# A new order of the work between batch 2's first score piece and its first feed-forward piece

## The chip, the cores and the metric

The kernel runs on one core of one Trainium2 chip. The metric is the device time of one execution in microseconds (us), smaller is better. A core has five engines with queues of their own: TensorE (PE, matrix products into PSUM; its weight loads are shown as PEld), VectorE (DVE), ScalarE (ACT), GpSimd (POOL) and SyncE (SP, which here only issues DMAs). Each takes its instructions in the order of the program and waits on semaphores for what the others make. PSUM has eight banks of 128 x 512 numbers in fp32.

## The reference

Four batches, eight heads, 768 tokens, 64 numbers per head. Attention, then a feed-forward layer over the heads side by side:

```python
scores = (q @ k.T) / 8                       # per batch and head
keep = causal                                # heads 0, 2, 6 ("retrieval")
keep = causal & (key < 4 | query - key < 64) # the other five ("streaming")
a = softmax(where(keep, scores, -1e9));  o = a @ v
x = o with its heads side by side            # 3072 tokens x 512
h = x @ w_in                                 # 512 x 2048
g = max(h, 0) + alpha * min(h, 0)
out = g @ w_out                              # 2048 x 512
```

## The kernel before

Products run in bf16 with fp32 sums. A batch's eight heads are four pairs, (2,6), (1,5), (0,4), (3,7), numbered n = 4 * batch + pair; batch 2 is n = 8 to 11. Tokens of the feed-forward layer come in tiles t of 512 and 256 in turn, two per batch: t = 4 and 5 belong to batch 2.

The program is one list of named items, `ORDER` (line 14). The loop at line 817 calls each item's function in that order, and so sets the order in every engine's queue; a planner wrote the list offline. An item is named by a letter, then n, head of the pair (0 or 1) and piece, or t and block:

- `Lq`, `Lk`, `Lv`: loads from HBM, issued by SP (two parts of Lk13 by POOL). `Cq`, `Ck`, `Cv`: casts to bf16, in batch 2 and later on DVE (lines 322, 341, 356). `Dq`, `Dk`: DMA transposes of the cast q and k, issued by SP (lines 329, 345).
- `S`: a score piece on PE; `s`: its exponential on ACT (lines 477, 524, 526); `m`: its mask by a product on DVE (lines 486, 535, 538). A retrieval head of batch 2 has six pieces of 448 columns, a streaming head two of 352 and one of 448.
- `A`: weights times v on PE (line 562), with the row sums; `a`: the division on DVE (lines 572, 573); `X`: a DMA transpose of the pair's result into `xT`, issued by SP (line 581).
- `P`: a piece of x @ w_in on PE, four matmuls of 512 columns or eight of 256 (line 607), the last in each sum reading the fourth pair's `xT`; `p`: ACT's relu into one of three `neg` buffers (line 612); `g`: DVE's product and sum that makes g (line 619; t even one instruction, t odd two).
- `O`: a quarter of g @ w_out for 128 tokens, four matmuls of 512 columns (line 627); `o`: ACT's copy (line 633) and the store, issued by POOL (line 637).

Score items that stand near one another are collected and emitted together (`emit_burst`, line 425). If each of the pair's heads has at least 576 columns in the collection, the heads go on the two halves of the array's rows and run side by side (line 438); otherwise each piece goes alone over all rows, against zeros in the other half (line 431). An item that `beside_burst` (line 442) does not let pass ends the collection.

PSUM banks are handed out in the list's order too: `take` (line 151) picks the bank that was given back longest ago, `give` (line 157) returns it. So another order gives other banks to the items, and a PE item waits until the bank's last reader has run.

In the stage that the change touches, PE does the last four P of t = 2 and 3, the scores and the `A` of batch 2, and the O of t = 2 and 3; the next item, P4.11, needs `xT` of n = 8 to 11. The loads and casts for batch 3 (n = 12 to 15) have begun.

Of the kernel before, what the change touches and what calls it, by code (L numbers as in the profile page):

```python
# [40 lines left out]
p2.9 P3.4 Ck9 Cq9 g2.9 P2.14 p2.14 g2.14 Cq8 p3.4 Lq10 Lq11 Dk8.0 P2.10 p2.10 Dk9.1 o1.0 p2.3  # L41
g2.3 g3.4 Dk8.1 P3.2 P3.14 P3.12 P2.8 Dq8 P2.1 P3.8 o1.1 p3.2 Dk9.0 Lv10 g2.10 Dq9 p3.14 P2.7
Ck10 g3.2 p3.12 g3.12 g3.14 P2.2 p2.2 g2.2 Cq10 Dq10 P2.11 p2.1 g2.1 p2.11 p2.8 g2.11 P3.6 P2.5
p2.5 g2.5 P2.13 p2.13 g2.8 g2.13 P2.0 p2.0 g2.0 p2.7 P3.0 p3.0 P2.4 S8.0.5 Lv8 Lv11 P2.15 P2.12
s8.0.5 Cq11 g3.0 p2.15 g2.7 g2.15 S8.0.0 p2.12 g2.12 Ck11 p3.6 S9.0.2 P2.6 p2.6 g3.6 s8.0.0 p2.4 g2.4
g2.6 s9.0.2 p3.8 P3.10 g3.8 p3.10 O3.0.0 O2.0.0 S8.1.5 s8.1.5 O3.0.1 O2.0.1 g3.10 m8.0.0 Cv8 S8.1.3 S9.0.0 S8.0.3
S9.1.1 S8.0.1 S9.1.0 s8.1.3 s9.1.0 s8.0.1 s9.0.0 s8.0.3 m8.0.3 m8.0.1 O2.0.2 O2.0.3 o2.0 Dk10.1 Lv9 m9.0.0 Cv9 m8.0.5
Dk11.0 m9.1.0 m9.0.2 S8.0.4 S9.0.1 S10.1.1 S8.1.4 Dq11 s8.1.4 Lq13 Lk13 O3.0.2 Dk10.0 s9.1.1 s10.1.1 s9.0.1 s8.0.4 O3.0.3
o3.0 Dk11.1 S10.1.0 S10.1.2 m9.0.1 S11.0.2 S9.1.2 S8.0.2 S11.0.0 s9.1.2 Cv10 m9.1.1 A9.0 s11.0.2 s10.1.0 O2.3.0 m9.1.2 A9.1
a9.0 a9.1 X9 s10.1.2 s11.0.0 O2.3.1 Lq15 Lv14 Lq12 S8.1.0 S11.0.1 S10.0.3 m10.1.0 s8.0.2 S10.0.1 S8.1.2 S8.1.1 S10.0.0  # L50
O2.3.2 s8.1.2 s8.1.0 m8.1.4 Cq13 s11.0.1 s8.1.1 m11.0.2 m10.1.2 m8.0.4 m11.0.0 A8.0 s10.0.0 m8.1.5 m10.1.1 O2.3.3 a8.0 S11.1.2
S10.0.4 S11.1.0 S10.0.5 S10.0.2 m8.1.3 m11.0.1 s10.0.3 s10.0.1 S11.1.1 s11.1.2 A10.1 s11.1.1 O2.2.0 O2.1.0 s10.0.4 m6.0.2 m10.0.1 Cv11
m8.1.1 m8.1.0 a10.1 m10.0.4 Ck13 m10.0.0 m11.1.2 A11.0 A8.1 O2.1.1 s10.0.2 s10.0.5 o2.3 s11.1.0 Dk13.0 m11.1.1 m10.0.3 m10.0.5
m11.1.0 A10.0 a11.0 a8.1 a10.0 O3.1.0 A11.1 Cq12 O2.2.1 O2.2.2 O2.2.3 a11.1 X8 O2.1.2 O3.1.1 O3.1.2 X10 o2.2
O3.1.3 O2.1.3 X11 P4.11 o2.1 P4.14 P5.14 p5.14 P4.4 P4.6 Lk12 P5.0 g5.14 Ck12 p4.4 p4.6 p4.11 P4.13
g4.6 p4.14 g4.11 Lq14 g4.14 P5.12 P4.5 P4.12 p4.13 Dq12 o3.1 p5.0 g4.13 Cq14 g5.0 Dk13.1 p4.5 g4.5
g4.4 Cv14 P4.9 p4.9 g4.9 P4.2 P5.2 Dq13 p5.12 g5.12 P4.10 p5.2 P4.8 P4.1 p4.12 g4.12 g5.2 p4.10
g4.10 Lv15 Dk12.0 Dk12.1 Lv12 p4.1 Lk14 Lv13 Lk15 g4.1 P4.7 P4.0 p4.2 g4.2 p4.8 g4.8 p4.0 p4.7
# [799 lines left out]
```

## Time and profile before

| what | value |
| --- | --- |
| median of 3 runs | 227.11 us (226.39 to 227.92) |
| profiled execution | 226.45 us |
| its span, first to last instruction | 224.7 us |
| changed stage, first score piece to P4.11 | 97.25 to 129.93 us of the span |

Times in the profile are us from the span's start, means of a group are ns. A timeline row is: start, us that the group took, engine and line, operation, what it writes and reads, shape, count. A q behind an engine's name means its sequencer, which issues DMAs. Matmuls overlap, so the end of one lies behind the start of the next; from start to start is what each costs PE. A `DMA_TRANSPOSE` row gives the time of issuing; the data land later.

### The profile page before, as it was taken

To read this page: it belongs to the slowest core of one execution; us is meant where nothing else is said; L and a number is where in the kernel's file an instruction comes from. 1 tells how busy PE (TensorE), PEld (TensorE's weight loads), DVE (VectorE), ACT (ScalarE), POOL (GpSimd) and SP (SyncE) were. 2 spreads that over 40 slices of the span, in tenths; PEclk is the share of its full clock that TensorE was granted. 3 is DMA by queue.
4 is the path that set the end of the run, shared out by engine and by line. 5 is a ranking of instruction groups with operands and counts; after the bars stand their busy time and mean duration, and the time that the engine had idled before them with its cause. 6 is when DMAs were issued, how large, how long until landed. Compare 5 with 4: busy or idle time off the path is not lost.

```text
span 224.7 us, 5206 instructions
## 1 busy us (share of the span) xinstructions
PE 220.6 (98%) x1986; PEld 135.7 (60%) x1986; DVE 148.4 (66%) x395; ACT 139.5 (62%) x286; POOL 45.0 (20%) x91
## 2 busy tenths in 40 slices
PE   7999999999999999999999999999999999999995
PEld 7989876575556557564556455556556455664454
DVE  5799648995579618898799029977589226866000
ACT  3788668999898037577993137787584237563311
POOL 4678769400230001000401001000110110000000
PEclk9999999999999999999999999999999999999999
DMA  6999999999999999999979898995721620000213
GB/s 194 309 235 203 272 218 266 220 196 202 221 233 233 160 248 217 187 172 202 240 164 183 218 238 195 191 161 115 126 95 39 152 96 0 0 1 3 91 63 128
DMA packets 96185, 37.58 MB, mean 167 GB/s; under 512 B 83208, under 2 KB 94368, under 8 KB 96160
## 3 DMA queue, kind: packets, MB, share of 16 engines
q1 hardware_dynamic: 89904, 27.92, 66.1%
q0 software_dynamic: 5792, 8.93, 18.0%
q10 hardware_dynamic: 464, 0.40, 0.6%
q8 instruction: 15, 0.25, 0.5%
q14 instruction: 10, 0.08, 0.1%
HBM read 27.71 MB, written 6.29 MB: 151 GB/s over the span
## 4 chain that ended last, share of the span: by engine, by line
PE 98%; DVE 0%; issue 0%; DVEq 0%
PE P L607 37%; PE P L627 36%; PE P L562 7%; PE P L438 4%; PE P L421 3%; PE P L698 3%; PE P L371 2%; PE P L646 2%; PE P L431 1%; PE P L508 1%; PE P L587 1%; PE P L470 0%; PE P L369 0%; DVE kT L394 0%; DVE ot L655 0%
## 5 line engine op out<-in xcount | busy, mean ns | idle before, releaser
L619 DVE SCALAR_TENSOR_TENSOR g<-neg,oma,P 128x256 bf16<-128x256 f32 (+1 forms) x128 | 71.0, 610 | 41.4 <-ACT neg L612 40.8
L607 PE MATMUL P<-xT,w_in_b 128*128 128x512 bf16 (+1 forms) x512 | 86.6, 326 | 0.0
L627 PE MATMUL P<-w_out_b,g 128*128 128x512 bf16 x368 | 85.1, 380 | 0.0
L612 ACT ACTIVATE neg<-P 128x512 f32<-128x512 f32 x96 | 54.2, 601 | 26.3 <-PE P L607 20.9
L607 PEld LDWEIGHTS <-w_in_b 128*128 128x128 bf16 x512 | 49.4, 98 | 32.4 <-DVE g L619 0.2
L627 PEld LDWEIGHTS <-g 128*128 128x128 bf16 x368 | 33.9, 98 | 37.4 <-issue 0.9
L477 ACT ACTIVATE eR<-P 128x448 bf16<-128x448 f32 (+3 forms) x63 | 35.9, 616 | 5.4 <-PE P L438 2.5
L633 ACT COPY ot<-P 128x512 f32<-128x512 f32 x23 | 13.8, 600 | 36.9 <-PE P L627 31.4
L637 POOL DMA_DIRECT2D out_dram<-ot x18 | 10.3, 572 | 110.2 <-ACT ot L633 110.0
L524 ACT ACTIVATE eS<-P 128x352 bf16<-128x352 f32 x45 | 20.5, 481 | 3.6 <-PE P L438 3.2
L573 DVE TENSOR_TENSOR xn<-P,rcp 128x448 bf16<-128x448 f32 (+1 forms) x32 | 19.1, 595 | 1.1
L535 DVE TENSOR_TENSOR eS<-eS,ms_near 128x352 bf16<-128x352 bf16 x45 | 14.7, 338 | 0.8 <-ACT eS L524 0.6
L486 DVE TENSOR_TENSOR eR<-eR,mr_near 128x128 bf16<-128x128 bf16 x54 | 10.9, 231 | 3.9 <-ACT eR L477 3.7
L421 PE MATMUL P<-qT,kT 128*128 128x192 bf16 (+14 forms) x68 | 11.2, 251 | 0.2 <-DVE kT L394 0.2
L562 PEld LDWEIGHTS <-eS 128*128 128x128 bf16 x266 | 9.8, 97 | 2.4 <-issue 0.6
L562 PE MATMUL P<-vb,eS 128*128 128x65 bf16 x266 | 11.0, 193 | 0.0
L572 DVE RECIPROCAL rcp<-P 128x7 f32<-128x7 f32 (+1 forms) x32 | 6.3, 196 | 6.6 <-PE P L562 6.0
L438 PEld LDWEIGHTS <-kT 64*128 64x128 bf16 x167 | 6.7, 94 | 6.1 <-issue 5.5
L438 PE MATMUL P<-qT,kT 64*128 64x176 bf16 (+7 forms) x167 | 10.3, 251 | 0.0
L562 PE MATMUL P<-vb,eR 128*128 128x65 bf16 x258 | 9.9, 193 | 0.0
L655 DVE COPY ot<-P 128x128 f32<-128x128 f32 x1 | 0.3, 292 | 14.3 <-PE P L646 14.3
L562 PEld LDWEIGHTS <-eR 128*128 128x128 bf16 x258 | 9.0, 97 | 1.1
(96 smaller groups left out, 175.0 us busy)
## 6 DMA issues: line engine op xcount, KB each, us to landing
out_dram<-ot POOLq DMA_DIRECT2D x18, 256.0 KB, 3.8
kf<-in_k_dram SPq DMA_DIRECT2D x21, 192.0 KB
qf<-in_q_dram SPq DMA_DIRECT2D x18, 192.0 KB
vf<-in_v_dram SPq DMA_DIRECT2D x14, 196.0 KB
qf<-in_q_dram SPq DMA_DIRECT2D x7, 384.0 KB
vf<-in_v_dram SPq DMA_DIRECT2D x12, 192.0 KB
w_in_b<-in_moe_w_in_dram POOLq DMA_DIRECT2D x8, 256.0 KB, 9.4
w_out_b<-in_moe_w_out_dram POOLq DMA_DIRECT2D x4, 512.0 KB, 13.3
```

Of the source, the lines that this page charges most:

```text
L421: nc.tensor.matmul(to, keys, queries, start=True, stop=stop)
L438: nc.tensor.matmul(to, keys[own], queries[own], start=True, stop=True)
L477: nc.scalar.activation(ebuf[n, hh][:, lo:hi].rearrange("p (x c) -> p x c", x=len(parts)), P[:, got[0]:got[0] + len(parts), 0:(hi - lo) // ...
L524: nc.scalar.activation(slots, sc[:, 0:352].rearrange("p (s c) -> p s c", c=176), AF.Exp, scale=scale)
L535: nc.vector.tensor_tensor(slots, slots, ms_near[:, 0:2, :] if m == 0 else ms_near[:, 1:3, :], op=ALU.mult)
L562: nc.tensor.matmul(pav[:, i, :], e[:, o:o + 128], vv[:, j, hh, 0:D + 1], start=(m == 0), stop=(m == len(terms) - 1))
L573: nc.vector.tensor_tensor(xn[n][:, 0:nt, D * hh:D * hh + D], pav[:, :, 0:D], rcp.to_broadcast([128, nt, D]), op=ALU.mult)
L607: nc.tensor.matmul(psg[:, w * i:w * (i + 1)], w_in_b[:, c, 128 * fb:128 * (fb + 1)], xT[:, c, o:o + w], start=(x == 0), stop=(x == 3))
L612: nc.scalar.activation(neg[t, f], bank(held["P", t, f][0]), AF.Relu, scale=-1.0)
L619: nc.vector.scalar_tensor_tensor(g_buf[t % 2][:, fb, 0:w], neg[t, f][:, c], oma[:, fb:fb + 1], bank(got[0])[:, c], op0=ALU.mult, op1=ALU.add)
L627: nc.tensor.matmul(bank(held["O", t, s][0]), g_buf[t % 2][:, f, 128 * s:128 * (s + 1)], w_out_b[:, f, :], start=(f == 0), stop=(f == 15))
L633: nc.scalar.copy(ot, bank(got[0]))
```

## The change

The list is changed from S8.0.5, the first score item of batch 2, to the last O ahead of P4.11: 188 items. Both lists hold the same items, each once, and the functions are the same. According to its description the order was sought by a planner that takes transposes and loads to land 1.5 (us) late. On PE the two lists read as follows, with score pieces that are emitted together in brackets and those side by side on the halves marked by "|":

```
before: [8.0.5] P2.15 P2.12 [8.0.0] [9.0.2] P2.6 P3.10 O3.0.0 O2.0.0 [8.1.5] O3.0.1 O2.0.1
  [9.0.0 8.0.3 8.0.1 | 8.1.3 9.1.1 9.1.0] O2.0.2 O2.0.3 [8.0.4 9.0.1 | 10.1.1 8.1.4] O3.0.2 O3.0.3
  [11.0.2 8.0.2 11.0.0 | 10.1.0 10.1.2 9.1.2] A9.0 O2.3.0 A9.1 O2.3.1
  [11.0.1 10.0.3 10.0.1 10.0.0 | 8.1.0 8.1.2 8.1.1] O2.3.2 A8.0 O2.3.3
  [10.0.4 10.0.5 10.0.2 | 11.1.2 11.1.0 11.1.1] A10.1 O2.2.0 O2.1.0 A11.0 A8.1 O2.1.1 A10.0 O3.1.0
  A11.1 O2.2.1 O2.2.2 O2.2.3 O2.1.2 O3.1.1 O3.1.2 O3.1.3 O2.1.3 P4.11
after:  [8.0.1] P2.6 P3.10 [9.0.0] P2.12 P2.15 O2.0.0 O2.0.1 O2.0.2
  [8.0.0 9.0.2 8.0.4 | 9.1.0 8.1.3 9.1.1] O2.0.3 O3.0.0 O3.0.1 O3.0.2 O3.0.3
  [9.0.1 8.0.3 8.0.2 | 8.1.1 9.1.2 8.1.0] O2.3.0 A9.0 O2.3.1
  [8.0.5 11.0.1 11.0.0 11.0.2 | 8.1.5 10.1.0 10.1.2] O2.3.2 O2.3.3 A9.1 O2.2.0 A8.0
  [10.0.1 10.0.3 10.0.0 | 8.1.4 10.1.1 8.1.2] O2.2.1 O2.2.2
  [10.0.5 10.0.4 10.0.2 | 11.1.0 11.1.2 11.1.1] A10.1 A8.1 O3.1.0 O3.1.1 A10.0 A11.1 A11.0
  O2.1.0 O2.2.3 O2.1.1 O2.1.2 O2.1.3 O3.1.2 O3.1.3 P4.11
```

SP issues in both lists Lv8, Lv11, Dk10.1, Lv9, Dk11.0, Dq11, Lq13, Lk13, Dk10.0, Dk11.1; then before X9, Lq15, Lv14, Lq12, Dk13.0, X8, X10, X11, and after Lq15, Lv14, Lq12, Dk13.0, X8, X9, X10, X11. The new lines:

```diff
+p2.5 g2.5 P2.13 p2.13 g2.8 g2.13 P2.0 p2.0 g2.0 p2.7 P3.0 p3.0 P2.4 S8.0.1 g3.0 P2.6 P3.10 p3.6
+Lv8 g2.7 S9.0.0 p2.4 Lv11 m6.0.2 g2.4 p2.6 s8.0.1 Dk10.1 P2.12 s9.0.0 P2.15 g2.6 O2.0.0 O2.0.1 m9.0.0 Lv9
+O2.0.2 S8.0.0 p3.8 g3.8 S9.0.2 p2.12 g2.12 S9.1.0 S8.1.3 p3.10 g3.10 S8.0.4 g3.6 p2.15 g2.15 S9.1.1 s9.1.1 Ck11
+s9.0.2 Cv10 Dk11.0 O2.0.3 Cq11 Dq11 O3.0.0 s8.1.3 O3.0.1 o2.0 Lq13 Lk13 s8.0.4 Dk10.0 Dk11.1 s8.0.0 s9.1.0 O3.0.2
+O3.0.3 o3.0 m9.0.2 S9.0.1 S8.0.3 m9.1.1 Lq15 S8.1.1 S9.1.2 S8.1.0 S8.0.2 s9.0.1 Cv9 s8.1.1 O2.3.0 m9.0.1 A9.0 m8.0.0
+O2.3.1 Lv14 Cv11 a9.0 S8.0.5 S11.0.1 s8.1.0 S11.0.0 m8.1.0 s9.1.2 S8.1.5 s8.0.3 S10.1.0 m9.1.2 m8.1.3 m8.1.1 s8.0.2 S10.1.2
+S11.0.2 s8.0.5 m8.0.3 s8.1.5 s10.1.0 O2.3.2 s11.0.2 O2.3.3 m8.0.5 Cv8 s11.0.1 m9.1.0 A9.1 m8.0.4 o2.3 O2.2.0 m8.0.1 A8.0
+s11.0.0 S8.1.4 S10.1.1 a9.1 s10.1.2 S10.0.1 S10.0.3 m10.1.2 S10.0.0 S8.1.2 s8.1.4 s10.0.3 s8.1.2 s10.0.0 m8.1.5 O2.2.1 a8.0 O2.2.2
+S10.0.5 m11.0.1 s10.1.1 S10.0.4 m10.1.0 s10.0.1 S10.0.2 S11.1.0 m11.0.2 S11.1.2 m10.0.3 Lq12 S11.1.1 s10.0.5 m10.1.1 A10.1 m8.1.4 m10.0.0
+A8.1 s11.1.0 Ck13 m11.1.0 m10.0.5 s11.1.2 m11.1.2 Dk13.0 a8.1 s10.0.4 X8 O3.1.0 m10.0.4 O3.1.1 m10.0.1 s10.0.2 s11.1.1 A10.0
+m11.1.1 X9 A11.1 m11.0.0 A11.0 a10.1 O2.1.0 O2.2.3 O2.1.1 o2.2 O2.1.2 a10.0 X10 a11.1 a11.0 X11 O2.1.3 Cq12
+Cq13 O3.1.2 O3.1.3 P4.11 o2.1 P4.14 P5.14 p5.14 P4.4 P4.6 Lk12 P5.0 g5.14 Ck12 p4.4 p4.6 p4.11 P4.13
```

More of the change, by code (lines that the diff above doesn't have):

```diff
@@ L43 @@
 Ck10 g3.2 p3.12 g3.12 g3.14 P2.2 p2.2 g2.2 Cq10 Dq10 P2.11 p2.1 g2.1 p2.11 p2.8 g2.11 P3.6 P2.5
[L44 to L52, printed above, removed]
@@ L53 @@
-m8.1.1 m8.1.0 a10.1 m10.0.4 Ck13 m10.0.0 m11.1.2 A11.0 A8.1 O2.1.1 s10.0.2 s10.0.5 o2.3 s11.1.0 Dk13.0 m11.1.1 m10.0.3 m10.0.5
-m11.1.0 A10.0 a11.0 a8.1 a10.0 O3.1.0 A11.1 Cq12 O2.2.1 O2.2.2 O2.2.3 a11.1 X8 O2.1.2 O3.1.1 O3.1.2 X10 o2.2
-O3.1.3 O2.1.3 X11 P4.11 o2.1 P4.14 P5.14 p5.14 P4.4 P4.6 Lk12 P5.0 g5.14 Ck12 p4.4 p4.6 p4.11 P4.13
+p2.5 g2.5 P2.13 p2.13 g2.8 g2.13 P2.0 p2.0 g2.0 p2.7 P3.0 p3.0 P2.4 S8.0.1 g3.0 P2.6 P3.10 p3.6
+Lv8 g2.7 S9.0.0 p2.4 Lv11 m6.0.2 g2.4 p2.6 s8.0.1 Dk10.1 P2.12 s9.0.0 P2.15 g2.6 O2.0.0 O2.0.1 m9.0.0 Lv9
```

## The prediction

> **What bounds the kernel now.** I read the page's head first: span, busy times, clock, chain.
>
> ```profile
> span 224.7 us, 5206 instructions
> PE 220.6 (98%) x1986; PEld 135.7 (60%) x1986; DVE 148.4 (66%) x395; ACT 139.5 (62%) x286; POOL 45.0 (20%) x91
> PEclk9999999999999999999999999999999999999999
> PE 98%; DVE 0%; issue 0%; DVEq 0%
> ```
>
> TensorE (PE) is busy 98% of the span, at the full granted clock in every slice, and the chain that ended last is PE's own queue. The profiled execution took 226.45 us: 224.7 of span and 1.75 around it, 0.66 below the median of 227.11.
>
> A busy PE could still hide gaps, because the ends of matmuls are modelled. So I read starts, in PE's timeline over the changed stage, from batch 2's first score piece (97.25) to its first feed-forward piece (129.93).
>
> ```profile
> 97.25 0.36 PE L431 MATMUL P<-qT,kT 128*128 128x64 bf16 x3
> 97.44 1.89 PE L607 MATMUL P<-xT,w_in_b 128*128 128x512 bf16 x8
> ...
> 105.06 0.71 PE L438 MATMUL P<-qT,kT 64*128 64x176 bf16 x12
> 105.70 1.90 PE L627 MATMUL P<-w_out_b,g 128*128 128x512 bf16 x8
> 107.53 0.52 PE L438 MATMUL P<-qT,kT 64*128 64x128 bf16 x8
> 107.98 1.90 PE L627 MATMUL P<-w_out_b,g 128*128 128x512 bf16 x8
> 109.82 0.71 PE L438 MATMUL P<-qT,kT 64*128 64x176 bf16 x14
> 110.46 0.57 PE L562 MATMUL P<-vb,eS 128*128 128x65 bf16 x13
> 110.87 1.03 PE L627 MATMUL P<-w_out_b,g 128*128 128x512 bf16 x4
> ...
> 113.08 0.90 PE L438 MATMUL P<-qT,kT 64*128 64x176 bf16 x11
> 113.91 1.04 PE L627 MATMUL P<-w_out_b,g 128*128 128x512 bf16 x4
> ...
> 116.38 0.75 PE L438 MATMUL P<-qT,kT 64*128 64x128 bf16 x13
> 117.05 0.63 PE L562 MATMUL P<-vb,eS 128*128 128x65 bf16 x15
> ...
> 123.03 7.07 PE L627 MATMUL P<-w_out_b,g 128*128 128x512 bf16 x32
> 129.93 5.25 PE L607 MATMUL P<-xT,w_in_b 128*128 128x512 bf16 x31
> ```
>
> From one group's start to the next is what the group costs. The last 32 matmuls of 512 columns take 129.93 - 123.03 = 6.90 us, 0.216 each, or four (a quarter O or a piece P) in 0.863. From 97.44, eight take 1.73. An AV of 13 matmuls takes 110.87 - 110.46 = 0.41. No row carries a wait, and the starts join without a hole: in 32.68 us I find no wait of PE. **So no wait can be taken out here**; the order can only change PE's own work, or bring waits in.
>
> The Trainium skill would let one doubt this. "TensorE: Matmul & The Clock Gate", section "Back-to-back issue gap", gives about 131 ns per 512-column matmul in a stream of weight loads and matmuls, and "Perfetto Trace Analysis", "Identifying the Most-Contended Engine", asks to judge headroom by weight-load busy time, here 60%. By the first, each 0.863 would hide 0.34 us. The trace speaks against it: 0.216 is the least step between these matmuls, with no wait before them.
>
> **The change part by part.** All 188 items of the stage stay, so every instruction is there as before, DMAs too. Only places change.
>
> *Score pieces in pairs.* Neighbouring score items are emitted together, head 0 and head 1 on the two halves of the array if each has 576 columns. A full-attention piece has 448 columns; a streaming one 352 (pieces 0 and 1) or 448 (piece 2). The longer half sets the time. Before, the five paired groups have longer halves of 1248, 800, 1248, 1696 and 1344 columns and take 0.64, 0.45, 0.64, 0.83 and 0.67 us by the rows above: 0.11 + 0.424 per thousand columns. After, there are again five, of 1344, 1344, 1600, 1344 and 1344 (the first is 8.0.0, 8.0.4, 9.0.2 against 9.1.0, 8.1.3, 9.1.1). The sum goes from 6336 to 6976 columns: +0.27. Each paired group also costs the work ahead of it 0.10 (eight O from 105.70 to 107.53 take 1.83, not 1.73), five times before and after; a group of 1344 so takes 0.78 in all. Unpaired remain 448 + 352 columns in place of four times 448, at 0.19 (97.44 - 97.25) per 448: 0.76 becomes 0.34, -0.42. **PE's work: -0.15 us.** All else on PE costs the same wherever it stands.
>
> *The start: does VectorE (DVE) keep up?*
>
> ```profile
> 94.67 2.72 DVE L619 SCALAR_TENSOR_TENSOR g<-neg,oma,P 128x512 bf16<-128x512 f32 x4
> 101.25 3.90 DVE L619 SCALAR_TENSOR_TENSOR g<-neg,oma,P 128x256 bf16<-128x256 f32 x8
> 95.71 1.70 ACT L612 ACTIVATE neg<-P 128x512 f32<-128x512 f32 x3 [0.27 <-PE P L607]
> ```
> ```profile
> L535 DVE TENSOR_TENSOR eS<-eS,ms_near 128x352 bf16<-128x352 bf16 x45 | 14.7, 338 | 0.8 <-ACT eS L524 0.6
> ```
>
> A g of 512 columns costs DVE 0.68; the second row holds three split ones and two whole, so a split one costs 0.85. PE now runs S8.0.1, P2.6, P3.10, S9.0.0, P2.12, P2.15 and three O2.0 by 97.25 + 0.19 + 0.15 + 7 x 0.863 = 103.6, and meets the first pair group there; before, it met its first at 105.06. Its last piece, S9.1.1, takes the PSUM bank that g3.6 gives back. On DVE, from 97.4, g3.0, g2.7, g2.4, g2.6, a mask, g3.8, g2.12, g3.10 and g3.6 come to 4 x 0.85 + 4 x 0.68 + 0.34 = 6.5, at 103.9; the three neg buffers make ACT wait for DVE now and then, and by following these relus through I add 0.3: 104.2. PE asks at 104.1 (0.1 of entry, two 176-wide matmuls and a piece of 448 ahead on that half). A wait of 0 to 0.3 us; I take 0.1. Behind it on PE all else waits. O2.0.3 needs g2.15 for its fourth matmul alone, at 103.6 + 0.78 + 0.65 = 105.0; g2.15 is done at 104.9. Covered by little: 0 to 0.2, I take 0.
>
> *The middle: transposes of item 11.* Ck11 moves behind g2.15 on DVE, and SyncE's (SP's) queue waits for it with Dk11.0, Dq11 and the loads Lq13, Lk13 behind.
>
> ```profile
> 73.38 5.11 SPq L581 DMA_TRANSPOSE xT<-xn  x3
> 97.86 2.04 SPq L345 DMA_TRANSPOSE kT<-natk  x1
> 101.95 1.27 SPq L345 DMA_TRANSPOSE kT<-natk  x1
> 103.32 1.23 SPq L329 DMA_TRANSPOSE qT<-natq  x1
> 122.10 4.23 SPq L581 DMA_TRANSPOSE xT<-xn  x3
> 126.38 1.16 SPq L253 DMA_DIRECT2D kf<-in_k_dram  x2
> ```
> ```profile
> 79.91 4.28 PE L607 MATMUL P<-xT,w_in_b 128*128 128x512 bf16 x23
> ```
>
> SP's rows are the time to issue; the page shows no landing for them. An upper bound: batch 1's last three xT transposes were issued by 78.49, and the piece that needs the last in its fourth matmul, at 79.91 + 0.65 = 80.56, did not wait; landing came at most 2.07 us after the issue's end, at least 0. In the new order Ck11 ends about 105.5, Dk11.0 and Dq11 end their issue at 108.0 (1.27 + 1.23), at worst at 109.6 (2.04 each), and land by 110.1 to 111.7. S11.0.1 asks at about 111.9: behind the first pair group (from 103.6, 0.78) come O2.0.3, four quarters of O3.0, a pair group, O2.3.0, A9.0 and O2.3.1, or 7 x 0.863 + 0.78 + 0.41 = 7.2, and in its own group 0.3 of entry and S8.0.5. **Cost 0**, cover 0.2 us at the bound and 1.8 with a landing at the issue's end. SP's earlier idle time costs nothing; Lq13 and Lk13 feed Cq13 and Ck13, some 10 us later.
>
> *The end of the scores.* From the fourth pair group PE does 0.78, two O, 0.78, A10.1 (15 matmuls at 0.41 / 13, 0.47), A8.1 (21, 0.66) and two O before A10.0: 6.1 us. ACT has eleven exponentials there.
>
> ```profile
> 114.88 1.88 ACT L477 ACTIVATE eR<-P 128x448 bf16<-128x448 f32 x4
> ```
>
> At 0.47 each, 0.15 for the second part of s11.1.2, and 0.45 until the first can start (entry, one piece, and 0.15 that I estimate for the hand-over): 5.8. A11.1, 0.65 later on PE, needs the twelfth and its mask: 6.6 against 6.75. A wait of 0 to 0.3 us; I take 0.05.
>
> *The tail: X11 under less cover.* P4.11 needs all four xT. Before, X8, X10 and X11 were issued by 126.33 and P4.11's fourth matmul came at 130.58. Now X9 no longer goes ahead alone at 113.2 but stands second of four in a row, and behind A11.0 come seven quarters of O (6.04 us); before, eight came behind A11.1. With P4.11 still near 129.95, A11.0 ends at 123.9. On DVE the last four outputs follow one another:
>
> ```profile
> 121.51 0.56 DVE L573 TENSOR_TENSOR xn<-P,rcp 128x384 bf16<-128x384 f32 x1
> 122.20 0.56 DVE L573 TENSOR_TENSOR xn<-P,rcp 128x384 bf16<-128x384 f32 x1
> ```
>
> At 0.7 apiece (122.20 - 121.51), from about 122.8 for a10.1, a11.0 ends at 125.6. SP reaches X8 when a8.1 is done, near 122.4, and at 4.23 / 3 = 1.41 each ends X11's issue at 128.0. It lands between 128.0 and 130.1, needed at 130.6. **Cost 0**, but 1.7 us of cover are spent. Lk12, next on SP, starts 1.7 later. Its user is Ck12 on DVE:
>
> ```profile
> 134.15 0.62 DVE L341 CAST natk<-kf 128x896 bf16<-128x896 f32 x1
> kf<-in_k_dram POOLq DMA_DIRECT2D x2, 7.0 KB, 4.1
> ```
>
> With 4.1 us to land, the only row for a load of k, its second half would be there at 132.8. Covered.
>
> **Sum:** -0.15 + 0.1 + 0 + 0.05 + 0 = 0.0. The profiled execution stays at 226.4 to 226.5, and the median at **227.1 us**. The three runs differ by 1.5 us, so under 1% (2.3 us) a measurement can hardly tell a change from none.
>
> **The rivals.** *Late transposes: slower.* For: X11 has 0.5 us of cover at the bound, Dq11 0.2, and SP's issue time has outliers, 2.04 against 1.27; at batch 1's mean of 5.11 / 3 = 1.70, X11 would end its issue at 129.2 and could land 0.7 too late. Should each of the four X take 2.04, X11 ends its issue at 130.6 and lands by 132.6: P4.11 waits 2.0 us, 229.1. It decides from X11 landing after 130.6. Against: batch 2's own three took 1.41 each, and the bound on landing is not what a landing takes. If Dq11 is late by 1.5 besides, 230.6. Chance 0.12.
>
> *DVE and ACT fall behind.* The three small waits at their upper ends: 0.3 + 0.2 + 0.3 - 0.15 = +0.65, 227.8. For: the covers are some 0.1 us; against: they were added up with the relus' waits in. Chance 0.2.
>
> *Hidden headroom.* If PE had room that its rows don't show, or if runs above the profiled one carry late DMAs that the new order bears better, up to 0.7 us (227.11 - 226.45) goes: 226.3. Since no wait stands in the trace, it gets 0.08. By the page's 131 ns the stage's 28 quarter O and P would hold 28 x 0.34 = 9.5 us, and up to 217.6 could be reached; against a step of 0.216 that never shrinks I give this 0.01, within the 0.08. The same holds for an order that bears delays of 1.5 us better but meets none: it ends as the forecast.
>
> **How the numbers follow.** Forecast, within 0.4 us of 227.1: 0.6; the others as given. The range runs from the headroom case, 226.2, to 228.5, which takes in the busy engines and the smaller delays and leaves out some 0.1 to 0.15. Slower by over 1% needs over 2.3 us of waits, the upper part of the first rival: 0.07. Faster by over 1% would need PE to do less: 0.02. Within: 0.91.
>
> **What would show it.** PE's starts again without holes over a stage 32.5 to 33 us long; five pair groups, the third the longest at 0.79; SP's four X in a row to about 128; PE at P4.11 without a wait. A wait ahead of S9.1.1 up to 0.3 shows the first term. The prediction is wrong if PE stands over 1 us, at P4.11 for xT or in the third pair group for qT, or if a later stage waits for Lk12's successors.

## The result and the profile after

The changed kernel takes 228.26 us (median of 12 runs, 227.15 to 229.84) against 226.69 us for the kernel before (12 runs, 226.16 to 228.24): ratio 1.0062, 95% interval 1.0034 to 1.0091, so about 1.4 us slower. A ratio, here and below, leaves out runs that fell in a slower state of the chip, while a median counts all runs of a kernel. Its profiled execution took 228.50 us, 226.8 of it span. The head of its page and the chain's shares:

```profile
span 226.8 us, 5207 instructions
...
PE 221.4 (98%) x1986; PEld 136.4 (60%) x1986; DVE 148.9 (66%) x395; ACT 139.7 (62%) x286; POOL 45.2 (20%) x91
...
PE 91%; DMA 3%; SPq 2%; ACT 2%; issue 1%; DVE 1%; DVEq 0%
```

PE's busy share still reads 98%. The last line is the telling one: before, the chain was PE for 98%; now it leaves PE for 3% of DMA and 2% of SP's queue. The waits of PE say where (line, releaser, us in all, times, longest):

```profile
PE P L438 <- DMA kT<-natk: 1.3, 1, 1.3
PE P L698 <- DVE busy L295: 1.2, 1, 1.2
```

The second is at the start of the program, outside the stage. The first is the only wait in the stage that the view names. PE's timeline of the stage, in the columns used ahead of the prediction:

```profile
97.88 0.35 PE L431 MATMUL P<-qT,kT 128*128 128x320 bf16 x2
...
104.38 0.92 PE L438 MATMUL P<-qT,kT 64*128 64x448 bf16 x12
105.23 4.49 PE L627 MATMUL P<-w_out_b,g 128*128 128x512 bf16 x20
109.65 0.75 PE L438 MATMUL P<-qT,kT 64*128 64x176 bf16 x11
110.33 1.04 PE L627 MATMUL P<-w_out_b,g 128*128 128x512 bf16 x4
...
112.56 0.86 PE L438 MATMUL P<-qT,kT 64*128 64x64 bf16 x18
113.35 1.90 PE L627 MATMUL P<-w_out_b,g 128*128 128x512 bf16 x8
...
116.34 0.80 PE L562 MATMUL P<-vb,eR 128*128 128x65 bf16 x21
118.42 0.74 PE L438 MATMUL P<-qT,kT 64*128 64x320 bf16 x10 [1.29 <-DMA kT<-natk]
119.10 1.90 PE L627 MATMUL P<-w_out_b,g 128*128 128x512 bf16 x8
120.93 0.75 PE L438 MATMUL P<-qT,kT 64*128 64x64 bf16 x13
121.61 0.63 PE L562 MATMUL P<-vb,eS 128*128 128x65 bf16 x15
...
131.91 2.27 PE L607 MATMUL P<-xT,w_in_b 128*128 128x512 bf16 x11
```

The stage now takes 131.91 - 97.88 = 34.03 us against 32.68, **1.35 more**, and one row carries it: the fourth paired group (8.1.4, 10.0.1 and their fellows) stands 1.29 us for a kT. From P4.11 to the end the two kernels take the same, 94.9 and 94.8 us. The rest of the difference of the two spans, 0.63 us, lies ahead of the stage (it starts at 97.88, not 97.25), where the lists are the same; it is no work of the change. Where a profile below has such an offset (the experiments e1, e2 and e8 have one of 2 to 4 us), stages are compared, not spans.

Which kT it is, and why so late, the chain tells in order of time (start, us, what):

```profile
108.71 0.58 SPq L219
...
109.34 0.65 SPq L219
...
110.04 0.96 SPq L246
...
111.04 1.21 SPq L246
...
112.29 6.09 DMA kT<-natk
...
118.42 0.74 PE P L438 x7
```

Ahead of the transpose stand the four loads of item 13, Lq13 and Lk13 (lines 219 and 246). The first transpose behind them is **Dk10.0**: 6.09 us from the start of its issue to its landing. SP's queue, after and then before:

```profile
102.47 0.43 SPq L249 DMA_DIRECT2D vf<-in_v_dram  x1
106.10 1.22 SPq L345 DMA_TRANSPOSE kT<-natk  x1
107.43 1.22 SPq L329 DMA_TRANSPOSE qT<-natq  x1
108.71 1.29 SPq L219 DMA_DIRECT2D qf<-in_q_dram  x2
110.04 2.21 SPq L246 DMA_DIRECT2D kf<-in_k_dram  x2
112.29 2.01 SPq L345 DMA_TRANSPOSE kT<-natk  x1
```
```profile
104.60 1.17 SPq L219 DMA_DIRECT2D qf<-in_q_dram  x2
105.81 1.12 SPq L246 DMA_DIRECT2D kf<-in_k_dram  x2
106.98 3.06 SPq L345 DMA_TRANSPOSE kT<-natk  x2
```

The order in the queue is that of before. But SP stands idle from 102.90 to 106.10, for Ck11; the four loads take 3.50 us to issue instead of 2.29; and Dk10.0, which before began its issue 9.73 us into the stage, begins it at 14.41. The page lists no landings, but the trace has the semaphore update at the end of each transfer, and from these the table is read (us from the stage's start):

| Dk10.0 | issue | landing | lag behind the issue's end | wanted by PE at |
| --- | --- | --- | --- | --- |
| before | 9.73 to 11.45 | 13.94 | 2.49 | 15.9 |
| after | 14.41 to 16.42 | 20.49 | 4.07 | 19.2 |

So PE wants it 3.3 us later than before and gets it 6.5 later.

### The profile page after: what moved, and what is told of

It is laid out like the page before. It is cut to its first block, busy times and chain, and to the rows that moved or that the text cites. A ratio compares the mean times of both kernels' runs of the same rounds, so it can differ in the third digit from the quotient of the medians.

```text
span 226.8 us, 5207 instructions
## 1 busy us (share of the span) xinstructions
PE 221.4 (98%) x1986; PEld 136.4 (60%) x1986; DVE 148.9 (66%) x395; ACT 139.7 (62%) x286; POOL 45.2 (20%) x91
## 4 chain that ended last, share of the span: by engine, by line
PE 91%; DMA 3%; SPq 2%; ACT 2%; issue 1%; DVE 1%; DVEq 0%
PE P L607 37%; PE P L627 32%; PE P L562 7%; PE P L438 4%; DMA kT<-natk 3%; PE P L698 3%; PE P L421 2%; PE P L371 2%; PE P L646 2%; PE P L431 1%; SPq L246 1%; ACT eR L477 1%; PE P L508 1%; PE P L587 1%; PE P L369 1%
## 5 line engine op out<-in xcount | busy, mean ns | idle before, releaser
L438 PE MATMUL P<-qT,kT 64*128 64x176 bf16 (+7 forms) x173 | 10.8, 250 | 1.3 <-DMA kT<-natk 1.3
```

The costliest lines, as they stand in the source:

```text
L438: nc.tensor.matmul(to, keys[own], queries[own], start=True, stop=True)
```

## The experiments

The theory (A in the expectations): the loss is one wait, for Dk10.0, and Dk10.0 is late because it stands on SP behind the stop for Ck11 and behind item 13's loads. The rivals: the late start of the stage's transposes is only a symptom, and the time is in other terms (the first group's bank, X11's lost cover, the DMA traffic of POOL). All edits are moves in the list, against the changed kernel unless said otherwise.

**e1.** Dk10.0 alone goes ahead of the stop:

```diff
-O2.0.2 S8.0.0 p3.8 ... Lq13 Lk13 s8.0.4 Dk10.0 Dk11.1
+Dk10.0 O2.0.2 S8.0.0 p3.8 ... Lq13 Lk13 s8.0.4 Dk11.1
```

> The changed order with one item moved: Dk10.0, the transpose whose late landing PE waited 1.29 us for at 118.42, is issued right behind Lv9, where SP stood idle from 102.9 to 106.1. Theory A (SP's queue: Ck11 late on DVE holds SP, and Dk10.0 stands behind it and four loads): Dk10.0 lands near 107, the wait ahead of S10.0.1 is gone, and the ratio to before falls from 1.006 to 0.998 to 1.001. Theory B (DMA traffic: any transpose issued among these loads and stores lands late): the wait moves to Dk11.0 or Dq11, which now start behind one transpose more, and the third pair group waits 0.5 us or more; ratio 1.003 or more. Theory C (the order itself asks PE for more than the old one did, the wait is only where it shows): the ratio stays above 1.004.

Measured: 227.29 against 227.29 us, ratio 1.0001 (0.9975 to 1.0027). The loss is gone. Dk10.0 lands 8.46 us into the stage, the stage takes 32.66 us, and in PE's timeline the fourth group follows A8.0 at once:

```profile
119.57 0.80 PE L562 MATMUL P<-vb,eR 128*128 128x65 bf16 x21
120.30 0.74 PE L438 MATMUL P<-qT,kT 64*128 64x320 bf16 x10
...
134.88 1.35 PE L607 MATMUL P<-xT,w_in_b 128*128 128x512 bf16 x6 [0.30 <-DMA xT<-xn]
```

From A8.0 to the group are 0.73 us; in the changed kernel 118.42 - 116.34 = 2.08, so the wait cost 1.35 net, the whole of the stage's growth. The last row shows what the wait had hidden: without it, P4.11's fourth matmul is 0.3 us too early for X11, which lands at 33.73.

**e2.** The loads go behind both transposes instead:

```diff
-Lq13 Lk13 s8.0.4 Dk10.0 Dk11.1 s8.0.0
+s8.0.4 Dk10.0 Dk11.1 Lq13 Lk13 s8.0.0
```

> The changed order with Lq13 and Lk13 issued behind Dk10.0 and Dk11.1 instead of ahead of them; Ck11 stays late on DVE. Theory A: Dk10.0 is issued near 108.7 instead of 112.3, lands by 113.5, and PE, which asks at 117.1, does not wait; ratio 0.998 to 1.001. If the late Ck11 alone were the cause and the four loads had no part in it, the wait would stay at over 0.8 us and the ratio at 1.004 or more. Cq13 and Ck13 have time: their loads come 3 us later and are read at 121.6 or later.

Measured: 232.18 us (median of six), ratio 1.0134 (1.0072 to 1.0196; it counts the runs of 228.92, 229.63 and 231.71): a miss. The wait for Dk10.0 is gone as foreseen (landing at 15.13, stage 32.66), but SP and its transfers are now behind for the rest of the stage (X11's issue ends at 33.53, against 31.17 in e1), and the X transposes at its end pay. PE's timeline at P4.11, and the window behind it (span, us, then busy us and count of PE, PEld, DVE, ACT, POOL, then the granted clock, DMA share, GB/s):

```profile
134.46 0.38 PE L607 MATMUL P<-xT,w_in_b 128*128 128x512 bf16 x1 [1.03 <-DMA xT<-xn]
136.80 9.53 PE L607 MATMUL P<-xT,w_in_b 128*128 128x512 bf16 x41 [1.96 <-DMA xT<-xn]
```
```profile
137.00:145.00 8.00, 7.95 (x32) 3.97 (x32) 2.24 (x5) 2.33 (x5) 0.00 (x0) 0.65 1.05 202
```

X10 and X11 land at 34.25 and 36.58; PE stands 1.03 + 1.96 us, and then has the clock at half for 6.83 us (135.82 to 142.65), which is some 3.4 us more. From P4.11 to the end are 101.0 us instead of 94.9. This profiled execution was the slowest of the six, 235.55 us; how much of these waits and of the half clock the three counted runs had, no trace shows. The backlog was only moved, and to a place with less cover.

**e3.** The stop itself is taken away, Ck11 and Cq11 cast early on VectorE:

```diff
-O2.0.2 S8.0.0 p3.8 ... s9.1.1 Ck11 ... O2.0.3 Cq11 Dq11
+O2.0.2 Ck11 Cq11 S8.0.0 p3.8 ... s9.1.1 ... O2.0.3 Dq11
```

> The changed order with Ck11 and Cq11 ahead of the first pair group, so that DVE makes them near 101.5 instead of 105.5 and SP goes on without a stop; SP's order stays. Theory A: Dk10.0 is issued near 109 and lands by 114.5, no wait for it. DVE's relu products come 1.0 us later, so S9.1.1 waits for g3.6's bank some 0.8 us longer: ratio 1.001 to 1.004. If the four loads ahead were the whole cause, the wait for Dk10.0 would still be there in part, and the ratio 1.006 or more.

Measured: 228.05 us, ratio 1.0041 (1.0009 to 1.0074). Dk10.0 lands at 15.20 and nobody waits for it; but the casts push the g of the relus back on VectorE, and PE's waits have a new line:

```profile
PE P L438 <- DVE g L619: 0.8, 1, 0.8
```

It is the bank of g3.6 ahead of S9.1.1, the wait that the prediction had at 0.1. The stage takes 33.43 us. One wait was exchanged for another, as expected.

**e4.** The opposite: in the kernel *before*, Ck11 alone is put late:

```diff
-g2.12 Ck11 p3.6
+g2.12 p3.6
-m8.0.0 Cv8
+m8.0.0 Ck11 Cv8
```

> The kernel before with one item moved: Ck11 on DVE from ahead of p3.6 (100.7) to behind m8.0.0 (105.3), as late as the changed order has it. Theory A: SP stands from 101.9 to 106; Dk11.0, Dq11, Lq13, Lk13 and Dk10.0 follow 4 us later than before. Dq11 lands near 111, S11.0.2 asks at 109.8: a wait of 1 to 1.5 us; Dk10.0 lands near 116 to 118, S10.0.3 asks at 113.1 plus that wait: 2 to 3 us more. In all +3 to +4.5 us, ratio 1.013 to 1.020. Theories B and C expect under 1 us, since neither the traffic nor PE's order is new.

Measured: 235.82 us (median of four), ratio 1.0309 (1.0237 to 1.0382; it counts the runs of 232.88, the profiled one, and 235.25), more than the 1.013 to 1.020 expected. The mechanism is made in the old order, where Dk10.0 is wanted 3.3 us sooner. PE's timeline, the chain's row of the transpose, and the window behind the wait:

```profile
113.58 0.36 PE L438 MATMUL P<-qT,kT 64*128 64x176 bf16 x3
118.19 1.30 PE L438 MATMUL P<-qT,kT 64*128 64x64 bf16 x8 [4.25 <-DMA kT<-natk]
```
```profile
112.00 6.15 DMA kT<-natk
```
```profile
118.00:123.00 5.00, 4.81 (x42) 2.31 (x44) 0.83 (x4) 3.13 (x7) 0.00 (x0) 0.66 1.10 222
```

The stage takes 38.87 us, 6.2 more than before: 4.5 us of waits and the half clock behind them (3.41 us, 117.95 to 121.36, some 1.7 us lost). The expectation had the wait and not the clock.

**e5.** The loads go into SP's idle time ahead of the stop:

```diff
-O2.0.2 S8.0.0 p3.8 ... o2.0 Lq13 Lk13 s8.0.4 Dk10.0
+Lq13 Lk13 O2.0.2 S8.0.0 p3.8 ... o2.0 s8.0.4 Dk10.0
```

> The changed order with Lq13 and Lk13 issued ahead of Dk11.0, into the stop that SP makes while it waits for Ck11; Dk10.0 keeps its place behind Dq11 and so is issued 3.5 us sooner. If what counts is SP's queue time alone, every transpose is as early as or earlier than in the changed order: Dk10.0 is issued near 10.8 us after the stage's start and lands by 15.5, no wait for it (PE asks at 19.2), the xT transposes are not later, and the ratio is 0.998 to 1.002. If a load right ahead delays what lands behind it, Dk11.0 and Dq11 land 1 us or more later than 11.2 and 13.5 after the stage's start, S11.0.1 (14.5) waits up to 1 us, and the ratio is 1.002 to 1.006.

Measured: 226.98 against 226.99 us, ratio 0.9996 (0.9976 to 1.0017). Dk10.0 lands at 14.57; Dk11.0 and Dq11, now behind the loads, land 1.0 and 0.2 later than in the changed kernel and are still in time. The stage takes 32.66. Its one wait is that of e1, at P4.11: 0.3 us for X11.

**e6.** e1, with X9 also issued early (behind O2.2.2), so that X11 has one transpose fewer ahead:

```diff
-O2.2.1 a8.0 O2.2.2 S10.0.5 ... m11.1.1 X9 A11.1
+O2.2.1 a8.0 O2.2.2 X9 S10.0.5 ... m11.1.1 A11.1
```

> The changed order with Dk10.0 right behind Lv9 as in the first experiment, and X9 ahead of Lq12 instead of behind X8, so that three transposes of xT and not four stand in a row at the end. X11 is issued some 1.2 us sooner and lands before P4.11's fourth matmul asks for it (in the first experiment it was 0.3 us late there). Stage 32.6 to 32.8 us, no wait at P4.11; ratio 0.997 to 1.000. If the four in a row are not what made X11 late, a wait of 0.2 to 0.5 us stays, ratio 1.000 to 1.002.

Measured: 226.79 against 226.99 us, ratio 0.9984 (0.9964 to 1.0004). The time fits, the reason given only in part: X11's issue ends at 30.25, 0.9 sooner than in e1, but it takes 3.22 us more to land and is there at 33.47. From start to start of the matmuls, P4.11's fourth comes 0.20 us late, against 0.46 in e1. (The waits of PE in e6 name 0.6 us for an xT; that one is at 81.16, ahead of the stage, and not of this edit.)

**e7 and e10.** The same kernel, run once (e7) and ten times (e10): the two stores of o2.0 and o3.0 are left out, so two blocks of the output are not written.

```diff
-        (nc.gpsimd if t < 6 else nc.sync).dma_start(out[r:r + 128, :], ot)
+        if (t, s) not in ((2, 0), (3, 0)):
+            (nc.gpsimd if t < 6 else nc.sync).dma_start(out[r:r + 128, :], ot)
```

> The changed order without the stores o2.0 and o3.0 (two of the 24 blocks of the output are not written; all else is done). In the changed order they move 0.5 MB at 107.4 and 110.6, while Dk10.0 waits its turn. If they are what makes Dk10.0 land 4.1 us after its issue ends instead of 2.5 as before, the wait ahead of S10.0.1 falls from 1.29 to under 0.3 us. If SP's late start and its loads are the cause, the wait stays at 0.9 us or more.

> The seventh kernel once more, timed: the changed order without the stores o2.0 and o3.0 (two blocks of the output are not written). If its one look was no accident, PE does not wait for Dk10.0 and the ratio to before is 0.998 to 1.003; if the stores have no part, it is 1.005 or more, as for the changed order.

Measured: e7 227.73 us in its one run; e10 227.18 against 227.00 us, ratio 1.0002 (0.9977 to 1.0027). PE does not wait for Dk10.0 in either (from A8.0 to the group 117.00 - 116.27 = 0.73 in e7). In e7's one run P4.11 waits 0.59 us for X11 instead, in e10 it does not. So the wait falls, as the first of e7's two branches said, but not for its reason, since the lag stays (below); that 0.9 us or more of the wait would stay is a miss. POOL's DMAs in the changed kernel, in the kernel before and in e10:

```profile
107.44 0.91 POOL L637 DMA_DIRECT2D out_dram<-ot  x1 [19.36 <-ACT ot L633]
108.34 1.27 POOL L249 DMA_DIRECT2D kf<-in_k_dram  x2
110.64 0.59 POOL L637 DMA_DIRECT2D out_dram<-ot  x1 [1.02 <-ACT ot L633]
```
```profile
108.52 0.54 POOL L637 DMA_DIRECT2D out_dram<-ot  x1 [21.07 <-ACT ot L633]
109.21 1.56 POOL L249 DMA_DIRECT2D kf<-in_k_dram  x2 [0.15 <-issue]
110.95 0.59 POOL L637 DMA_DIRECT2D out_dram<-ot  x1 [0.19 <-issue]
```
```profile
87.18 1.41 POOL L249 DMA_DIRECT2D kf<-in_k_dram  x2 [0.15 <-issue]
```

In the changed kernel POOL's DMAs go out while SP issues item 13's loads (108.71 to 112.25); before, they went out when those were through (106.93). The edit moves more than the stores: item 13's small k loads stand behind the first store on POOL, and with it gone they leave 20 us sooner. With both out of the way, SP issues its four loads in 2.3 us again, and the two transposes behind them in 2.9:

```profile
107.66 1.16 SPq L219 DMA_DIRECT2D qf<-in_q_dram  x2
108.86 1.12 SPq L246 DMA_DIRECT2D kf<-in_k_dram  x2
110.03 2.92 SPq L345 DMA_TRANSPOSE kT<-natk  x2
```

Dk10.0 lands at 18.7 (e7) and 18.8 (e10), 1.7 us sooner. Its lag behind the issue's end stays, at 3.94 and 4.06 us, so that part does not come from POOL's DMAs. The Trainium skill, "DMA: Bandwidth & Descriptors", section "Issuing engines are not separate DMA queues", says that DMAs started by different engines share the same DMA engines, and that spreading them saves only sequencer time. The runs agree that the queues are not independent, and add that the sequencer's own time suffered here: a pair of k loads took SP 1.12 us beside nothing of POOL's and 2.21 beside it. POOL is not the only thing that lengthens it: the four loads took 3.6 us in e2 and 3.0 in e5 while POOL issued nothing.

**e8 and e9.** e5 with X9 early as in e6, and the same with the store o2.2 moved behind P4.11:

```diff
-O2.2.1 a8.0 O2.2.2 S10.0.5 ... m11.1.1 X9 A11.1
+O2.2.1 a8.0 O2.2.2 X9 S10.0.5 ... m11.1.1 A11.1
-O2.1.1 o2.2 O2.1.2 ... O3.1.3 P4.11 o2.1
+O2.1.1 O2.1.2 ... O3.1.3 P4.11 o2.2 o2.1
```

> The changed order with Lq13 and Lk13 in SP's stop, as in the fifth experiment, and X9 ahead of Lq12, where that experiment left SP idle for 2.3 us (20.8 to 23.0 after the stage's start) until Ck13. So nothing behind X9 starts later, and X11 is issued about 1 us sooner than in the fifth. If X11's place in SP's queue sets its landing, it lands by 32.7 after the stage's start, PE asks at 33.3, no wait at P4.11; ratio 0.996 to 0.999. If something beside it (the store o2.2, issued at 29.4) sets it, X11 still lands at 33.4 or later and the wait of 0.2 to 0.6 us stays.

> As the eighth, with o2.2 (copy and store of 256 KB) behind P4.11, so that no store runs beside the xT transposes. If the store delays them, X11 lands 0.7 to 1.5 us after its issue ends less late than in the eighth (there 2.5 to 3.2 after the end), and the wait at P4.11 is gone for sure; ratio 0.996 to 0.999. If not, both are alike within 0.001.

Measured: e8 227.24 against 227.00 us, ratio 1.0002 (0.9968 to 1.0036); e9 226.85, ratio 0.9984 (0.9955 to 1.0012). On ACT and POOL nothing stands between the two places of o2.2, so the store left as before and e9 is a repeat of e8; it says nothing on the store. In both the stage is free of waits and 32.66 us long, and X11 lands at 31.27 (e8) and 32.54 (e9). So X11 came in time, as e8's first branch said, but e8's ratio is not under 0.999. In e9's timeline of PE:

```profile
116.22 0.80 PE L562 MATMUL P<-vb,eR 128*128 128x65 bf16 x21
116.95 0.74 PE L438 MATMUL P<-qT,kT 64*128 64x320 bf16 x10
...
130.42 0.81 PE L607 MATMUL P<-xT,w_in_b 128*128 128x512 bf16 x3
```

This is the new order with every wait taken out, and it ends where the kernel before ends. No version tried beats the kernel before by more than its interval.

What is shown: the loss is the wait for Dk10.0 (e1), and that wait is a sum against its cover. Taking away any one of the stop (e3), the loads ahead (e2, e5; in e1 the stop too) or POOL's DMAs beside them (e7, e10) is enough to end it.

Why the transpose's lag was 4.07 us here and 2.49 before is in part open. It was 3.6 to 4.1 behind the loads in e3, e4, e7 and e10, and 2.3, 2.9 and 1.6 with no load just ahead (e1, e2, e5), but before has the loads ahead too. The landings say where the difference lies. In all twelve traces the full-size transfers of SP (those with 16 updates of their semaphore) land in the order of their issue. The last load ahead landed 1.9 us after Dk10.0's issue ended in both kernels (at 13.36 before, at 18.32 after); Dk10.0 landed 0.6 us behind it before and 2.2 behind it after. So the 1.6 us more do not come from the loads ahead; they lie between the last load's landing and Dk10.0's. There, at 18.08, the changed kernel's trace has a packet of 16 KB that it calls "instruction" (queue q8, 15 of them in a run). Every one of the twelve traces has one between 15.2 and 18.8 us of the stage, and there one transfer lands 1.8 to 2.7 us behind the one ahead of it; half of the other transfers that stood in the queue near there land within 0.9 us of the one ahead. Before, it met Dk11.1 (2.4), which PE did not wait for. That this packet holds the transpose up is argued, not shown: no run moves it, and e3's Dk10.0 landed 2.05 behind its load without one.

## Why the prediction was wrong, point by point

The forecast of no change missed a small loss; 228.26 is 1.16 us above the forecast and inside the range, and +0.62% is inside the 1% that was called hard to tell.

**The step that failed** is the end of the middle part: "SP's earlier idle time costs nothing; Lq13 and Lk13 feed Cq13 and Ck13, some 10 us later". Behind SP's stop it followed Dk11.0, Dq11 and the two loads, and ended there. Dk10.0 and Dk11.1 stand behind those loads in the same queue and have a user on PE; neither was priced.

**Naming it would not have been enough.** By the prediction's own terms, from the changed stage's start: its 108.0 for the end of Dq11's issue is 10.75 (measured 10.77, so this step was exact). Add 2.29 for the loads, 1.53 for the transpose (half of 3.06) and the bound of 2.07 for the landing: 16.6, wanted at 19.2. A cover of 2.6 us, cost 0. Measured against that:

| term for Dk10.0 | by the rows of before | measured | more |
| --- | --- | --- | --- |
| issue of Lq13, Lk13 | 2.29 | 3.50 | 1.2 |
| issue of Dk10.0 (before: 1.72 by its own row) | 1.53 | 2.01 | 0.5 |
| issue's end to landing | up to 2.07 | 4.07 | 2.0 |

With 0.1 us between issues, 3.8 us more against 2.6 of cover is the wait of 1.3. Two things were taken for constants: the issue time, where POOL's DMAs now fall beside the loads, and the landing. "Landing came at most 2.07 us after the issue's end" was one transfer's bound carried over to all. The trace of before refutes it, at Dk10.0 itself: 2.49 us, by the semaphore update at its end, which the prediction took to be unknown.

**PE's work, -0.15: right.** The paired groups take, start to start, 0.85, 0.68, 0.79, 0.68 and 0.68 us in the rows of the result; forecast were 0.68 for a group of 1344 columns and 0.79 for the third. The first holds the wait ahead of **S9.1.1**, which the trace lets go when a g of DVE ends: 0.17, forecast 0.1 in 0 to 0.3. e3 shows that the step was real: 0.8 as soon as VectorE has more to do. Without the wait for Dk10.0 the stage takes 32.66 (e1, e5, e8, e9) against 32.68 before, which is the sum of 0.0. **Dq11** was in time, as forecast: it landed at 13.52, and the third paired group began at 14.68. (The cover of 1.8 us "with a landing at the issue's end" was misnamed: 111.9 - 110.1 goes with the faster issue and the landing at its bound.) **The end of the scores** cost nothing, forecast 0.05. Its 0.15 for the hand-over to ACT came from no row; the whole term, from the group's start to the first exponential, was 0.41 for 0.45.

**The tail** was right for the changed kernel only by chance. X11 ended its issue 32.24 us into the stage and landed at 34.68, just when the delayed P4.11 wanted it; the forecast had issue's end at 128.0, 30.8 into the stage. With the stage's wait gone it came 0.3 late (e1, e5), lag 2.55 and 2.79: again the landing term.

**The rivals.** "Late transposes" had the right kind (0.12), but at X11 and Dq11, and at 2.0 us instead of 1.3. "DVE and ACT fall behind" did not come; e3 had to be built to bring it out. Hidden headroom: e9, with no wait left, is level with before, and four matmuls of 512 columns still take 0.86 us; nothing of the 131 ns that the prediction weighed shows.

## What to carry to other kernels

When a wait stops a DMA queue, list every transfer behind the stop up to the queue's next idle time, each with its user on the bound engine, not just the first few. Price a transfer's landing from its own semaphore updates under like traffic, counted from the landing of the transfer ahead of it in the queue, and ask which other queue's transfers will now go out beside it. Here, with PE without a wait in the stage before, the new order had next to nothing to win and a cover to lose at each transfer; to undo such a loss, use the queue's idle time (e5) rather than pushing its backlog towards the end (e2).

## What the runs showed of the hardware

- Issuing a load is not a fixed price: SP's four loads took 2.3 us in the kernel before, e3, e7 and e10, and 3.5 beside POOL's DMAs in the changed kernel, but also 3.6 in e2 and 3.0 in e5 with POOL issuing nothing. Transposes of k took 1.2 to 2.8 us to issue.
- Dk10.0 landed 1.6 to 4.1 us after its issue's end in the ten variants, and X11 of one and the same order on SP 1.56 us after it in e8 and 2.54 in e9. Full-size transfers of SP landed in the order of issue in all twelve traces.
- A wait of PE can cost more than itself. After 4.25 us idle the clock was half for 3.41 us (e4); after 1.03 and 1.96 us, with one matmul between, for 6.83 us (e2). In e1, ahead of the stage, a single wait of 1.94 us was followed by 3.41 us at half (31.95 to 35.37 of the span), while at the same place 1.87 us in e8 and 2.18 in e2 were not. After the 1.29 us of the changed kernel nothing was lost: its trace has no record of the clock, but eight matmuls of 512 columns behind the wait took 1.83 us (119.10 to 120.93), as before. The Trainium skill, "TensorE: Matmul & The Clock Gate", section "HAM oscillation — how this bites in real kernels", puts the limit at idle gaps above some 3.4 us. e4 agrees; in e1 one gap and in e2 two gaps, each below that limit, were enough.
